# Decays computed sequence by sequence, B loaded in halves, fillers rearranged, and two gathers moved, in a fused scan and expert kernel

## The chip, the core and the metric

The kernel runs on one core of a Trainium2 chip. The metric is the device time of one execution in microseconds (us), median of several runs. The profiled execution comes with a span, from the first to the last instruction, which is a little shorter than the device time.

## What is computed

Two blocks stand one behind the other. The first is a selective state-space scan over 4 sequences, 8 heads, 768 positions, head size 32 and state size 16; the second sends each of the 3072 tokens to one of 8 experts by a hash of its id.

```python
# scan, per sequence b and head h, in chunks along the positions
cum   = cumsum(log(clip(a, 1e-6, 1)))            # inside a chunk
M     = (C @ B.T) * exp(cum_i - cum_j) * causal
y     = M @ x + (C @ state) * exp(cum_i)
state = exp(cum_last) * state + sum_j exp(cum_last - cum_j) * B_j x_j
# bridge: tokens are (b, position), features are (head, head_dim), so 3072 x 256
e     = token_id * 2654435761 % 8
out   = relu(y @ w1[e]) @ w2[e]                  # w1 256 x 1024, w2 1024 x 256
```

## The kernel before

All of the order is written by hand (`tc.manual_schedule`): each engine executes its instructions in the order in which the program names them, so a waiting instruction holds back everything behind it on that engine.

**Start.** The decays `a` of all four sequences come in one transfer (L90) into `a_t`, 96 partitions by 32 rows (sequence, head) by 8 positions. Behind it on the queue of SyncE come B and C of sequence 0 (`load_bc(0)`, L97, tile `bc`), x of sequence 0 (`load_x(0)`, L110, tile `xall`, two transfers) and B and C of sequence 1. While these land, GpSimd builds masks, VectorE and ScalarE put zeros in the unused halves of `xall` (`clear_x`, L150), and TensorE multiplies constants (`spin`, L193, tile `y_ps`), which keeps it active. Then the decay chain runs once for all four sequences: clamp (L386, VectorE), logarithm (L388, ScalarE), running sum (L392, VectorE), a small matmul (L397), an addition (L399), two exponentials (L401 and L402, giving `fac`), and an expansion for the steps (`totx`, L411, GpSimd). The factors `step` and `step2` come from `steps()` (L435): four small matmuls and three exponentials, called inside `turn_b(0)`.

**Scan.** For each sequence, `rows` multiplies B or C by its factors (on VectorE for sequence 0, L465, and on GpSimd for the others, L469); `turn_b` and `turn_c` transpose the result on TensorE (L499) and copy it out of PSUM on ScalarE (L505, L512, L515); `turn_c` also builds `cp` on GpSimd (L522). `turn_steps` transposes B back in blocks (L482; `bs`). `states` multiplies by x (L538) and carries the state forward on VectorE (L543, L547). `blocks` spreads the states over heads (L562). `grams` (L574, masked by `causal` into `m` on VectorE, L578) and `outputs` (L590, L597) give 128 tokens at a time, which ScalarE copies (L600) and SyncE writes to the tensor `y_tokens` (L601). The loop over `gc` (L638, 24 steps, 6 for each sequence) takes one output block per step and puts between them the preparation of the next sequence. `clear_x` for sequences 1 and 2 runs on ScalarE at steps 3, 5, 9 and 11 (L664). The routing (which expert, which place) is a generator `routing()` (L235); `next(todo)` puts one piece of it into the order of VectorE, a few per step (L665). It reads small tables that GpSimd fills (`tabs`, `keyc`, the `iota` tiles, L419 to L433).

**Experts.** The last steps of the scan gather the first two tiles of tokens (`gather_first`, L620, at step 17) and transpose them (`turn_x`, L616, at steps 22 and 23). Expert group 0 is then computed directly (`up` L854, `down` L865), while GpSimd gathers the tokens of the next groups (L605, tile `xg`) and forms sums of weights (`add_weights`, L736, tile `s`), `turn_next` transposes the gathered tokens (L884, copied by ScalarE into `xT`, L731), and `mix_x` (L761, tile `xmix`, VectorE) prepares group 1. Groups 1 to 7 use a scheme with seven products in place of eight (L795, L824). Results are transposed (L874) and scattered to the output (L713). The lines L900 to L920 order the passage into group 1.

Of the kernel before, what the change touches and what calls it, by code (L numbers as in the profile page):

```python
# [20 lines left out]
def kernel(  # L21
# [68 lines left out]
    nc.sync.dma_start(out=a_t, in_=a.rearrange("b h (p r) -> p (b h) r", r=RS))  # L90
# [3 lines left out]
    def load_bc(b):  # L94
        t = aload.tile([NR, 2, H, RS, NS], F32, name="bc")
        for i, src in ((0, B), (1, C)):
            nc.sync.dma_start(out=t[:, i].rearrange("p h r n -> p h (r n)"),  # L97
                              in_=src[b].rearrange("h (p r) n -> p h (r n)", r=RS))
        bcs[b] = t
# [16 lines left out]
    load_bc(0)  # L116
    load_x(0)
    load_bc(1)

# [24 lines left out]

    ident = const.tile([P, P], F32)
    make_identity(nc, ident)
    ones = const.tile([P, P], F32)
    nc.vector.memset(ones, 1.0)

    def clear_x(i, q, scalar):  # L150
        o = xall[q * HL:(q + 1) * HL, i, :, :, 1 - q].rearrange("j h k d -> j (h k) d")
        if scalar:
            nc.scalar.activation(o, ones[q * HL:(q + 1) * HL, 0:1].unsqueeze(2).to_broadcast([HL, G * NU, D]), AF.Copy, scale=0.0)  # L153
        else:
            nc.vector.memset(o, 0.0)

    clear_x(0, 0, False)
    scrap = const.tile([P, 1], F32)
    nc.scalar.activation(scrap, ones[:, 0:1], AF.Ln)
    clear_x(0, 1, True)  # L160
# [28 lines left out]
    turn0 = const.tile([NR, BH, RS], F32)  # L189
    nc.vector.memset(turn0, 1.0)  # L190
    nc.vector.memset(turn0[:, :, 0:1], 0.0)

    def spin(n, width=2):  # L193

        t = ps_y.tile([P, 512], F32, name="y_ps")
        for _ in range(n):
            nc.tensor.matmul(out=t[:, 0:width * P].rearrange("p (w i) -> p w i", w=width), lhsT=ident,
# [37 lines left out]
    def routing():  # L235
# [4 lines left out]
        nc.vector.tensor_scalar(out=eid_i, in0=tok[:, :, 0], scalar1=E - 1, scalar2=None, op0=OP.bitwise_and)  # L240
        eid_r = route.tile([NCH, P], F32)
        nc.vector.tensor_copy(out=eid_r, in_=eid_i)
        e_ps = ps_g.tile([P, 2, 512], F32, name="gram")[:, 0, 0:NCH]
# [119 lines left out]
        for c in range(NCH):  # L363
# [18 lines left out]
    next(todo)  # L382
    spin(2)


    nc.vector.scalar_tensor_tensor(out=a_t, in0=a_t, scalar=1e-6, in1=ones[0:NR, 0:1].unsqueeze(2).to_broadcast([NR, BH, RS]),  # L386
                                   op0=OP.max, op1=OP.min)
    nc.scalar.activation(a_t, a_t, AF.Ln)  # L388
    next(todo)
    cum = apre.tile([NR, BH, RS], F32)  # L390
    flat = lambda t: t.rearrange("p c r -> p (c r)")
    nc.vector.tensor_tensor_scan(out=flat(cum), data0=flat(turn0), data1=flat(a_t), initial=0.0,  # L392
                                 op0=OP.mult, op1=OP.add)
    next(todo)
    tot = cum[:, :, RS - 1]
    rel_ps = ps_t.tile([P, 512], F32, name="tp")
    nc.tensor.matmul(out=rel_ps[0:NR, 0:BH], lhsT=rel_w.rearrange("p k r -> p (k r)"), rhs=tot, start=True, stop=True)  # L397
    rel = apre.tile([NR, BH, RS], F32)
    nc.vector.tensor_tensor(out=rel, in0=cum, in1=rel_ps[0:NR, 0:BH].unsqueeze(2).to_broadcast([NR, BH, RS]), op=OP.add)  # L399
    fac = apre.tile([NR, 2, BH, RS], F32)  # L400
    nc.scalar.activation(fac[:, 0], rel, AF.Exp, scale=-1.0)  # L401
    nc.scalar.activation(fac[:, 1], rel, AF.Exp)  # L402
    next(todo)
    spin(2)

# [3 lines left out]
    nc.vector.memset(step2, 0.0)  # L409

    nc.gpsimd.tensor_copy(out=totx, in_=tot.unsqueeze(2).to_broadcast([NR, BH, NS]))  # L411
# [3 lines left out]
                            compare_op=OP.is_ge, fill=0.0, base=0, channel_multiplier=-1)  # L415
    nc.gpsimd.tensor_copy(out=causal[HL:P], in_=causal[0:HL])


    tabs = route.tile([P, 2, V], F32)  # L419
    for v in range(V):  # L420
        nc.gpsimd.memset(tabs[:, 0, v:v + 1], float(CAP - CAPS[v]))
        nc.gpsimd.memset(tabs[:, 1, v:v + 1], float(BEG[v] - 1 - (CAP - CAPS[v])))

# [683 lines left out]
```

## Time and profile before

Median of three runs: 255.59 us (253.53 to 255.78). The profiled run took 253.97 us, with a span of 252.2 us at a mean granted TensorE clock of 0.983.

| engine | busy us | share of the span |
|---|---|---|
| TensorE, matmul (PE) | 239.0 | 95% |
| TensorE, weight load (PEld) | 220.6 | 87% |
| VectorE (DVE) | 167.8 | 67% |
| GpSimd (POOL) | 135.7 | 54% |
| ScalarE (ACT) | 111.8 | 44% |

TensorE is the engine that sets the time. In a view of the profile by stages, it is busy for the whole of nearly every stage from 24 us on, until about 230 us. Where it is less busy, or runs at a lower clock, are the first 24 us: of 0 to 6 us it is busy 4.34, of 6 to 12 us 4.42, and of 18 to 24 us 4.58 us. (Some of that is the constant multiplication of `spin`.) A busy share says nothing on the clock: the profile gives the granted TensorE clock of each stage separately, 1.00 being the full one.

The transfers of the start, in order of their issue on SyncE, with the time from issue to landing that the profile gives for each:

| transfer | KB | issued at us | us to landing | landed at us |
|---|---|---|---|---|
| a, all sequences | 96 | 0.80 | 3.8 | 4.6 |
| B, sequence 0 | 384 | 1.25 | 5.7 | 7.0 |
| C, sequence 0 | 384 | 3.17 | 5.8 | 9.0 |
| x, sequence 0, first half | 384 | 3.75 | 7.0 | 10.8 |
| x, sequence 0, second half | 384 | 4.5 | 9.7 | 14.2 |
| B, sequence 1 | 384 | 8.71 | 7.7 | 16.4 |
| C, sequence 1 | 384 | 11.04 | 6.7 | 17.7 |

### The profile page before, as it was taken

The numbers are of one execution on the slowest core, as the hardware profiler recorded it, in microseconds if no ns is written. First come the engines' busy times: TensorE is split into PE (matmuls) and PEld (weight loads), VectorE is DVE, ScalarE is ACT, GpSimd is POOL, SyncE is SP. The second block draws the span as 40 slices with busy tenths as digits, with TensorE's granted clock in tenths as the row PEclk, the third lists the DMA queues.
The fourth block names the chain that finished last, engine by engine and source line by source line (L and its number), as shares of the span: only waits on it lengthen the run. The fifth ranks groups of instructions, "written<-read, shape, count | busy, mean of one in ns | idle before, by whom it ended". The sixth has DMA issues, their size and how long they took to land.

```text
span 252.2 us, 6781 instructions
## 1 busy us (share of the span) xinstructions
PE 239.0 (95%) x2615; PEld 220.6 (87%) x2615; DVE 167.8 (67%) x378; ACT 111.8 (44%) x256; POOL 135.7 (54%) x207
## 2 busy tenths in 40 slices
PE   6798999999999999999999999999999999999990
PEld 4676888888887788999999999999999999999970
DVE  6866488698652058676974994996787697784400
ACT  6643887965441325424334344343443453342120
POOL 6683290955303984279348629908937925504043
PEclk9987999999999999999999999999999999999998
DMA  6976899987872129242551642354164241001011
GB/s 115 160 122 116 131 201 189 248 196 233 249 256 67 60 92 312 71 168 62 171 209 42 208 166 83 119 173 147 47 209 184 62 169 39 21 4 40 21 44 60
DMA packets 50837, 33.21 MB, mean 132 GB/s; under 512 B 29753, under 2 KB 47186, under 8 KB 50804
## 3 DMA queue, kind: packets, MB, share of 16 engines
q1 hardware_dynamic: 47024, 24.22, 36.9%
q0 software_dynamic: 2400, 6.43, 8.1%
q10 hardware_dynamic: 1380, 2.12, 2.6%
q8 instruction: 21, 0.34, 0.6%
q14 instruction: 12, 0.10, 0.1%
HBM read 26.47 MB, written 6.42 MB: 130 GB/s over the span
## 4 chain that ended last, share of the span: by engine, by line
PE 73%; issue 11%; DVE 5%; ACT 4%; POOL 3%; DMA 1%; POOLq 1%; ACTq 0%
PE o_ps L824 20%; PE sum L795 12%; PE rest L795 6%; PE gram L574 5%; PE y_ps L590 5%; PE y_ps L597 4%; PE more L795 3%; PE tp L482 3%; PE o_ps L865 3%; POOL out_dram L713 2%; PE tp L499 2%; PE tp L538 2%; PE turns L884 2%; PE turns L874 2%; DMA a_t<-in_a_dram 1%
## 5 line engine op out<-in xcount | busy, mean ns | idle before, releaser
L713 POOL DMA_INDIRECT out_dram<-o_sb,idx_out x25 | 25.9, 1038 | 64.2 <-ACT o_sb L731 59.0
L824 PE MATMUL o_ps<-mixed,s 128*128 128x210 f32 (+6 forms) x168 | 37.0, 331 | 0.0
L605 POOL DMA_INDIRECT xg<-y_tokens,idx_in x25 | 26.4, 1058 | 18.5 <-ACT hd L725 12.0
L824 PEld LDWEIGHTS o_ps<-mixed,s 128*128 128x128 f32 x168 | 27.9, 190 | 0.0
L522 POOL TENSOR_TENSOR cp<-ct,step 128x256 f32<-128x256 f32 x24 | 13.9, 613 | 22.4 <-ACT ct L512 22.4
L731 ACT ACTIVATE u<-sum 128x420 f32<-128x420 f32 (+6 forms) x28 | 14.0, 501 | 23.6 <-PE sum L795 22.9
L795 PE MATMUL sum<-xmix,s 128*128 128x210 f32 (+6 forms) x112 | 23.5, 332 | 0.0
L736 DVE TENSOR_TENSOR mixed<-hT,mixed 128x420 f32<-128x420 f32 (+6 forms) x28 | 21.1, 754 | 0.5
L736 DVE TENSOR_TENSOR hT<-u,rest 128x420 f32<-128x420 f32 (+6 forms) x28 | 15.8, 564 | 7.7 <-PE rest L795 7.4
L578 DVE TENSOR_TENSOR m<-gram,causal 128x512 f32<-128x512 f32 x24 | 16.4, 685 | 5.9 <-PE gram L574 5.9
L808 DVE SCALAR_TENSOR_TENSOR mixed<-hT 128x420 f32<-128x420 f32 (+6 forms) x28 | 18.2, 691 | 1.0
L795 PEld LDWEIGHTS sum<-xmix,s 128*128 128x128 f32 x112 | 18.3, 189 | 0.6 <-issue 0.5
L731 ACT ACTIVATE o_sb<-turns 128x256 f32<-128x256 f32 x23 | 8.8, 384 | 20.5 <-PE turns L874 20.5
L600 ACT ACTIVATE y_sb<-y_ps 128x256 f32<-128x256 f32 x24 | 9.3, 388 | 17.9 <-PE y_ps L597 14.4
L597 PE MATMUL y_ps<-xall,m 128*64 128x64 f32 x384 | 16.8, 227 | 0.1
L574 PE MATMUL gram<-ce,bt 32*64 32x128 f32 x384 | 16.8, 288 | 0.0
L736 DVE TENSOR_TENSOR hT<-p,more 128x420 f32<-128x420 f32 (+6 forms) x14 | 7.9, 564 | 13.2 <-PE more L795 13.2
L731 ACT ACTIVATE xT<-turns 128x256 f32<-128x256 f32 x23 | 8.8, 384 | 17.2 <-PE turns L884 17.2
L590 PE MATMUL y_ps<-up,cp 128*64 128x128 f32 x176 | 16.2, 292 | 0.0
L731 ACT ACTIVATE p<-sum 128x420 f32<-128x420 f32 (+6 forms) x14 | 7.0, 501 | 20.3 <-PE sum L795 20.3
L597 PEld LDWEIGHTS y_ps<-xall,m 128*64 128x64 f32 x384 | 15.5, 141 | 0.6 <-ACT xall L153 0.6
L469 POOL TENSOR_TENSOR rows<-bc,fac 96x256 f32<-96x256 f32 x24 | 15.5, 675 | 0.8 <-DMA bc<-in_B_dram 0.7
(218 smaller groups left out, 581.5 us busy)
## 6 DMA issues: line engine op xcount, KB each, us to landing
w1odd<-in_moe_w_dram SPq DMA_DIRECT2D x8, 512.0 KB, 4.3
w2odd<-in_moe_w_dram SPq DMA_DIRECT2D x8, 512.0 KB, 4.4
y_tokens<-y_sb SPq DMA_DIRECT2D x24, 128.0 KB, 4.1
w1even<-in_moe_w_dram SPq DMA_DIRECT2D x6, 512.0 KB, 5.0
w2even<-in_moe_w_dram SPq DMA_DIRECT2D x6, 512.0 KB, 4.6
xall<-in_x_dram SPq DMA_DIRECT2D x12, 192.0 KB, 4.4
bc<-in_B_dram SPq DMA_DIRECT2D x4, 384.0 KB, 5.6
bc<-in_C_dram SPq DMA_DIRECT2D x4, 384.0 KB, 6.7
```

The costliest lines, as they stand in the source:

```text
L469: eng.tensor_tensor(out=t.rearrange("p r (h n) -> p h r n", h=H)[:, h:h + 2], in0=bcs[b][:, i, h:h + 2], in1=fac[:, i, hs].unsqueeze(3).to ...
L574: nc.tensor.matmul(out=gram[q * HL:(q + 1) * HL, g, u * P:(u + 1) * P], lhsT=bts[b][rr, 2 * c + u], rhs=ces[b][rr, :, 2 * c + u], start=Tr ...
L578: nc.vector.tensor_tensor(out=m.rearrange("p g u e i -> p g (u e i)"), in0=gram[:, :, 0:2 * P], in1=causal.rearrange("p (g x) i -> p g (x ...
L590: nc.tensor.matmul(out=y_ps[u * HL:(u + 1) * HL, :, q], lhsT=cps[b][:, q, k], rhs=ups[b][:, k].rearrange("p g (e d) -> p (g e) d", e=2), s ...
L597: nc.tensor.matmul(out=y_ps[u * HL:(u + 1) * HL, h], lhsT=m[:, g, u, e], rhs=xs[b][:, h, k], start=(k == 0 and h == 0), stop=(h == G - 1), ...
L605: nc.gpsimd.indirect_dma_start(out=dst, out_offset=None, in_=y_dram[0:n, :], in_offset=bass.IndirectOffsetOnAxis(ap=idx, axis=0), bounds_c ...
L713: st = nc.gpsimd.indirect_dma_start(out=out[:], out_offset=bass.IndirectOffsetOnAxis(ap=idx, axis=0), in_=src, in_offset=None, bounds_chec ...
L731: nc.scalar.activation(o, i, AF.Copy)
L736: eng.tensor_tensor(out=o, in0=i, in1=j, op=op)
L795: nc.tensor.matmul(out=self.banks[name][:, e * n:(e + 1) * n], lhsT=wt, rhs=mv, start=start and e == 0, stop=True, skip_group_check=True)
L808: nc.vector.scalar_tensor_tensor(out=t[:, o], in0=h[:, i], scalar=0.0, in1=h[:, k], op0=OP.max, op1=OP.subtract)
L824: nc.tensor.matmul(out=oP[v][o][:, e * n:(e + 1) * n], lhsT=wt, rhs=mv[:, c * n:(c + 1) * n], start=(j == 0 and c == 0 and i in (1, 3, 6, ...
```

## The change

The change has five parts. (1) `a` is loaded and turned into factors in three pieces: sequence 0, sequence 1, and sequences 2 and 3. The first piece goes ahead of everything, the others behind B and C of sequence 0 and behind B and C of sequence 1. The decay chain becomes a generator, `decays`, run for each piece; the clamps of the later pieces are on GpSimd. `steps` is called for each piece too. (2) B of sequence 0 is loaded in two halves by position, so that `rows` can begin on the first. (3) One activation table with logarithm and exponential is loaded at the start. (4) TensorE's fillers use a tile that is ready earlier, come as two groups of three, and two short ones are put between the first transposes; one `clear_x` goes from ScalarE to GpSimd, half of `cp` of sequence 0, the tables of the routing, and the second half of the states of sequence 0 go later in the order (the tables are filled behind the clamp of sequences 2 and 3, where the diff has `next(dec[2])` ahead of the loop). (5) At the passage to the experts, the first two token tiles are transposed one step earlier, the fourth tile of group 1 is transposed after the last `up`, and two gathers for group 2 are issued between the two halves of GpSimd's sums.

```diff
+    def load_a(b0, b1, eng):
+        eng.dma_start(out=a_t[:, b0 * H:b1 * H], in_=a[b0:b1].rearrange("b h (p r) -> p (b h) r", r=RS))
-    nc.sync.dma_start(out=a_t, in_=a.rearrange("b h (p r) -> p (b h) r", r=RS))
+    load_a(0, 1, nc.sync)
...
-            nc.sync.dma_start(out=t[:, i].rearrange("p h r n -> p h (r n)"),
-                              in_=src[b].rearrange("h (p r) n -> p h (r n)", r=RS))
+            n = RS // 2 if (b, i) == (0, 0) else RS
+            for r in range(0, RS, n):
+                nc.sync.dma_start(out=t[:, i, :, r:r + n].rearrange("p h r n -> p h (r n)"),
...
     load_bc(0)
+    load_a(1, 2, nc.sync)
     load_x(0)
     load_bc(1)
+    load_a(2, NB, nc.sync)
...
     clear_x(0, 0, False)
-    scrap = const.tile([P, 1], F32)
-    nc.scalar.activation(scrap, ones[:, 0:1], AF.Ln)
-    clear_x(0, 1, True)
+    nc.scalar.preload_act_table_set("natural_log_exp_and_others")
...
-            nc.tensor.matmul(out=t[:, 0:width * P].rearrange("p (w i) -> p w i", w=width), lhsT=ident,
+            nc.tensor.matmul(out=t[:, 0:width * P].rearrange("p (w i) -> p w i", w=width), lhsT=ones,
...
+    def decays(b0, b1):
...
+        eng = nc.gpsimd if b0 else nc.vector
+        eng.tensor_scalar(out=a_t[:, bh], in0=a_t[:, bh], scalar1=1e-6, scalar2=1.0, op0=OP.max, op1=OP.min)
+        yield
+        nc.scalar.activation(a_t[:, bh], a_t[:, bh], AF.Ln)
+        yield
+        nc.vector.tensor_tensor_scan(out=flat(cum[:, bh]), data0=flat(turn0[:, 0:n]), data1=flat(a_t[:, bh]), initial=0.0,
+                                     op0=OP.mult, op1=OP.add)
+        yield
+        tot = cum[:, bh, RS - 1]
+        rel_ps = ps_y.tile([P, 512], F32, name="y_ps")
+        nc.tensor.matmul(out=rel_ps[0:NR, 0:n], lhsT=rel_w.rearrange("p k r -> p (k r)"), rhs=tot, start=True, stop=True)
+        nc.gpsimd.tensor_copy(out=totx[:, bh], in_=tot.unsqueeze(2).to_broadcast([NR, n, NS]))
+        yield
+        nc.vector.tensor_tensor(out=rel[:, bh], in0=cum[:, bh], in1=rel_ps[0:NR, 0:n].unsqueeze(2).to_broadcast(sh), op=OP.add)
+        nc.scalar.activation(fac[:, 0, bh], rel[:, bh], AF.Exp, scale=-1.0)
+        nc.scalar.activation(fac[:, 1, bh], rel[:, bh], AF.Exp)
...
+    dec = {b: decays(b, min(2 * b, NB) if b else 1) for b in (0, 1, 2)}
+    next(dec[0])
+    next(dec[0])
+    next(todo)
+    next(dec[0])
+    next(dec[0])
+    next(todo)
+    next(dec[0], None)
+    spin(3)
...
+    next(dec[1])
     nc.gpsimd.tensor_copy(out=causal[HL:P], in_=causal[0:HL])
+    clear_x(0, 1, False, nc.gpsimd)
...
             if (b, i, r0) == (0, 0, RS // 2):
-                steps()
+                spin(1, 1)
+            elif (b, i, r0) == (0, 1, 0):
+                steps(0, 1)
+                next(todo)
+            elif (b, i) == (0, 1):
+                spin(1, 1)
...
+    next(dec[1])
     turn_c(0, True)
     next(todo)
     turn_steps(0, 0)
+    next(dec[1])
+    next(todo)
     grams(0)
-    states(0, 0)
+    next(todo)
+    states(0, 0, lambda: [next(dec[1], None) for _ in range(2)])
     blocks(0, 2, UH + 1)
     turn_steps(0, 1)
+    next(todo)
     rows(1, 0, nc.gpsimd)
+    put_steps(0, 8)
     rows(1, 1, nc.gpsimd)
+    next(dec[2])
...
-        if gc == 0:
-            states(0, 1)
+        if gc == 1:
+            steps(1, 2)
+        elif gc == 7:
+            steps(2, NB)
...
-                turn_b(nb)
+                turn_b(nb, (lambda: states(0, 1)) if b == 0 else None)
...
-        for _ in range((1, 2, 1, 0, 1, 0, 2, 2, 2, 0, 1, 0, 2, 2, 2, 1, 1, 0, 0, 1)[gc] if gc < 20 else 0):
+        for _ in range((1, 0, 0, 2, 1, 1, 2, 2, 2, 0, 1, 0, 2, 2, 2, 1, 1, 0, 0, 1)[gc] if gc < 20 else 0):
             next(todo, None)
+        if 0 < gc < 5:
+            next(dec[2], None)
...
-        elif gc > 21:
-            turn_x(gc - 22, (ps_t, "tp", 512), nc.vector.tensor_copy)
+        elif 20 < gc < 23:
+            turn_x(gc - 21, (ps_t, "tp", 512), nc.vector.tensor_copy)
...
-    for j in range(2):
-        take(add_weights(1, j, 0), 4)
+    take(add_weights(1, 0, 0), 4)
+    for k in new_tiles(2)[:2]:
+        gather(k)
+    take(add_weights(1, 1, 0), 4)
...
     for i in range(FP):
         up(0, i)
+        if i == 7:
+            turn_next(next(xs1))
+            mix_x(1)
         if i > 2:
             down(0, i - 3)
-        for _ in range((0, 0, 0, 0, 1, 1, 2, 0)[i]):
+        if 3 < i < 7:
             turn_next(next(xs1))
         if i == 5:
-            for k in new_tiles(2):
+            for k in new_tiles(2)[2:]:
                 gather(k)
-        if i == 6:
-            mix_x(1)
```

## The prediction, made before the change was run

> **What bounds the kernel now.** I read the stages first, then the chain that ended last, then the waits of the engine that sets the time. From 24 to 230 us TensorE is busy nearly throughout; time can only be won in front of that stretch, in its few gaps, or in its clock. The view by stages (us, then busy time and instruction count of PE, PEld, DVE, ACT and POOL, granted clock, DMA share, GB/s) shows two stretches at half clock:
>
> ```profile
> 10.00:11.00 1.00, 0.77 (x9) 0.59 (x8) 0.96 (x4) 0.85 (x4) 0.72 (x7) 1.00 1.27 178
> ...
> 13.00:14.00 1.00, 1.00 (x23) 0.88 (x20) 0.56 (x1) 1.00 (x3) 1.00 (x2) 0.50 1.15 187
> ...
> 19.00:20.00 1.00, 0.52 (x14) 0.42 (x14) 0.07 (x1) 0.36 (x2) 1.00 (x2) 1.00 0.00 0
> ...
> 23.00:24.00 1.00, 1.00 (x20) 0.94 (x16) 0.93 (x6) 0.00 (x0) 0.00 (x0) 0.50 0.78 127
> ```
>
> The chain of waits of the start (start us, length us, what) says what TensorE was late for:
>
> ```profile
> 0.80 3.76 DMA a_t<-in_a_dram
> 4.59 0.42 DVE a_t L386
> ...
> 7.14 0.43 ACT fac L401
> 7.60 1.06 DVE rows L465
> ...
> 13.36 1.06 PE gram L574 x16
> 14.42 1.15 PE tp L538 x48
> ...
> 17.61 0.48 DVE bs L485
> ...
> 19.90 0.49 PE tp L499 x4
> ```
>
> Decays until 7.57, transposes and copies until 13.36, states at 14.42, and a gap before the transposes of sequence 1 at 19.90. The chain does not name the transfers that arrived just in time: the second half of x landed at 14.2 us, and the first use of it (L538) is at 14.35; B of sequence 1 landed at 16.4 and its `rows` began at 16.56. ScalarE's timeline in the loop is nearly closed:
>
> ```profile
> 27.20 0.38 ACT L600 ACTIVATE y_sb<-y_ps 128x256 f32<-128x256 f32 x1 [1.00 <-PE y_ps L597]
> ...
> 34.60 0.39 ACT L600 ACTIVATE y_sb<-y_ps 128x256 f32<-128x256 f32 x1 [0.34 <-PE y_ps L597]
> 35.01 1.48 ACT L153 ACTIVATE xall<-ones 64x1536 f32<-64x1536 f32 x1
> ```
>
> Its clearing ends at 36.49 and the outputs of step 6 begin at 36.54: here ScalarE, not TensorE, ends the chain. Last, TensorE's waits from 60 to 110 us are three in all (engine, line, waited for: us, times, longest):
>
> ```profile
> PE turns L884 <- ACT xT L731: 0.9, 2, 0.5
> PE sum L854 <- DVE xT L618: 0.5, 1, 0.5
> ```
>
> **What the Trainium skill says.** "TensorE: Matmul & The Clock Gate", section on the HAM clock gate: the array's clock is halved unless recent activity was high, judged in free-running windows of about 3.4 us. The trace agrees on the halving and the length (11.81 to 15.02, 21.93 to 25.14), not on a simple busy share: PE was busy 2.82 us in the 3.4 us before the first, 2.17 between 5.0 and 8.4, and only the former was followed by half clock. "ScalarE: Activation LUTs", section on table sets: one set holds both exponential and logarithm. The trace shows two loads of 1.28 us each, of which the second (5.47 to 6.75) ended before `rel` was ready at 7.12. "DMA: Bandwidth & Descriptors", section on small descriptors: a fixed 3 cycles per packet, 11 cycles for 256 B. That makes 22 against 19 for two halves of 512 B, 16% (an estimate; no row here has 256 B pieces). "SBUF — State Buffer", section on who interferes with whom: an instruction of VectorE with two inputs contends with a GpSimd instruction that reads, not with one that only writes. So a clearing moved to GpSimd should leave VectorE's multiplications alone; no run so far shows it.
>
> **The change part by part.**
>
> *The first factors.* The pieces of `a` are 32 B long and took about 1.8 us of transfer (some 65 GB/s from 2.0 to 3.8 us, where B begins). A quarter takes 0.45, so it lands 1.35 earlier, at 3.2 in place of 4.56. The chain then has four times less per instruction. From the rows (0.42, 0.42, 0.69, 0.35, 0.42, 0.43 at 256 elements) and small ones of the same kind (0.17 to 0.21), I estimate clamp 0.2, logarithm 0.24, sum 0.29, matmul 0.3, addition 0.2, exponential 0.24, with gaps 0.2: 1.7, so factors at 4.9 in place of 7.57. The single table hides nothing new now, but keeps the shorter chain from meeting the second load. So the decay chain alone gains 2.7.
>
> *Does that reach TensorE?* B of sequence 0 comes 1.35 earlier for the missing `a`, less 16% of its 1.7 us of transfer, 0.3: 5.9 in place of 6.95, and its first half 1 us before that. C also comes about 1.0 earlier, at 8.0. `rows` of C then run 8.0 to 9.6, the transposes end near 10.2, and `ct`, which ended at 12.28, near 10.7. So the two grams and the first half of `bs` are ready by 12. But L538 needs x. On the queue in front of x stands half of `a` less than before (-0.9), and the halves of B (+0.3): x lands at 13.6 in place of 14.2 (bounds: 13.3 with no cost of the halves, 14.2 if they cost 0.9). **So only 0.6 of the 2.7 pass**, and B of sequence 1 likewise comes at 15.8 in place of 16.4. The clear (1.4 on GpSimd by its 64x512 memset of 0.52), behind the masks and the clamp of sequence 1 (0.2 to 0.35, which waits until about 8 for its piece), ends near 10.5, before any output.
>
> *Sequence 1.* GpSimd needs 2.75 from the start of `rows` to the fourth instruction (1.33 and three of 0.48 in the trace), so from 15.9 to 18.6, and TensorE's transposes follow at 18.7. Putting the second states behind the first batch of them lets TensorE use the rows at once; before, the copy of `bs` at 17.61 and a gap of 0.71 put them to 19.90. The group is L499 0.5, L538 0.7, L499 0.4: the gram of step 2 comes at 20.3 at full clock, at 21.0 to 21.6 if half clock falls on it, in place of 21.51. The outputs of step 0 are done near 17, so TensorE waits some 1.7 us ahead of 18.7, and so I count on half clock until about 21.9, as long as before but 3.3 earlier. Then the outputs of step 1 end at 22.9 in place of 24.13: 1.2 gained.
>
> *ScalarE in the loop.* It gets three exponentials for `step` (0.5 by L441 and L444: 0.21, 0.41), the logarithm for sequences 2 and 3 (0.29), and their two exponentials (0.56): 1.35. Half of it goes before step 2, where it waited 1.00 for TensorE; so `y_sb` of step 2 begins at 22.9 + 2.5 = 25.4, 1.8 earlier than 27.20. The exponentials of step 4 replace the wait of 0.34. **At the outputs of step 6 the start has gained 1.8**; at full clock throughout it would be 2.2, as ScalarE then has no gap left.
>
> *A new wait.* `keyc` is filled only behind `rows` of sequence 1 (8 times 0.48, plus 0.85), two pieces of `cp` (1.2), a clamp (0.3) and 18 memsets (0.6): near 22.8. VectorE's `key` waits for it, and `m` of step 2 is queued behind, done near 24.4. The outputs that need it come at 25 if step 1 ends at 22.9: nothing; at full clock it costs the rest above 2.2.
>
> *The passage.* The early `turn_x` lets VectorE's copy go beside the outputs of step 23: 0.5 (0.52 in the trace). The fourth `turn_next` behind the last `up` takes away one of the two waits on ScalarE's copy: 0.5 (0.47). `xmix` then is ready at 90.9 less 0.5, ahead of L795 at 92.18 less 1.0. The gathers of group 1 land 2.7 to 3.5 us from issue, the first at 82.4, and its transpose would stand at 82.78 less 0.5: no wait, or 0.1. The two early gathers hold the second sums by 2.6 us, to 92.6, while these are used at about 104: nothing. **Sum here 1.0.** The seven groups and the end stay as they are, bound by TensorE.
>
> Forecast: 255.6 - 1.8 - 1.0 = **252.8 us**.
>
> **Rivals.** (B) The fillers hold the clock, and the landings move by more than 0.6, since the queue is relieved also of the waiting behind it: B of sequence 1 a further 1.2 earlier, half clock 0.6 less: 252.8 - 1.8 = 251.0. For it: 4.5 us of one queue's issue time go into x alone; against: x is bound by its 128 B pieces (786 KB from 7.4 to 12.7 us), which stay. (C) A transfer that is hidden anyway: halves of B cost 0.9, x lands at 14.2 as before, B of sequence 1 too, and only the order (0.2) and the passage (1.0) gain: 254.4. For it: x at 14.2 against its use at 14.35; against: 48 KB less of the smallest pieces ahead of it. (D) Slower: the additions to ScalarE lie in full on the closed stretch (+1.35), and VectorE's wait for `keyc` delays `m` (+0.9, if GpSimd's contention stretches its rows), with nothing from the start and the passage's 1.0: 256.8. For it: the closed timeline above; against: the 1.00 gap in it.
>
> **How the numbers follow.** Forecast 0.5, B 0.25, C 0.17, D 0.08. The likeliest is 252.8. The range goes from B, with 0.2 for a full clock, to C, with 0.5 for a first gather that TensorE waits for: 250.8 to 254.9. Faster by over 1% means under 253.03: all of B and six tenths of the forecast, 0.55. Slower by over 1% would need D twice over: 0.06. The rest, 0.39, is within 1%.
>
> **What would show it.** The first exponential done near 4.9; L538 starting when x lands, near 13.6; `rows` of sequence 1 at 15.9; half clock in one stretch around 18.7 to 21.9; the outputs of step 6 at 34.7; no wait of L854 on `xT`, and one in place of two of L884. It is wrong if x lands no earlier, if VectorE's `key` holds up `m`, or if TensorE waits at a place that the trace before does not show.

## The result, and the profile after

The changed kernel takes **257.44 us** (median of 6 runs, 256.43 to 258.29), the kernel before in the same comparison 254.95 us (6 runs, 253.53 to 255.78). The ratio is **1.0104**, 95% interval 1.0064 to 1.0144: slower by some 2.5 us, where 252.8 us and a gain were forecast. The profiled execution has a span of 255.8 us, against 252.2. In some executions every one of these kernels runs slower as a whole; the ratios leave these out, the medians do not, and each group of experiments has its own timing of the kernel before (medians from 253.19 to 253.90 us).

The view by stages of the changed kernel (us, then busy time and instruction count of PE, PEld, DVE, ACT and POOL, granted clock, DMA share, GB/s), in the stretches that were shown of before:

```profile
10.00:11.00 1.00, 0.76 (x28) 0.62 (x25) 0.94 (x3) 0.97 (x4) 0.92 (x2) 1.00 1.63 141
...
13.00:14.00 1.00, 0.91 (x22) 0.57 (x25) 0.64 (x2) 0.00 (x0) 0.74 (x2) 0.50 1.17 224
...
18.00:19.00 1.00, 1.00 (x12) 1.00 (x13) 0.97 (x4) 1.00 (x4) 1.00 (x3) 0.50 0.03 8
19.00:20.00 1.00, 1.00 (x16) 0.93 (x15) 1.00 (x2) 0.22 (x2) 1.00 (x2) 0.72 0.00 0
...
23.00:24.00 1.00, 1.00 (x28) 0.96 (x26) 0.03 (x1) 0.84 (x5) 0.94 (x23) 1.00 0.43 70
```

Half clock now comes in one stretch from 12.73 to 19.56, as long as the two of before together (11.62 to 15.03 and 21.86 to 25.27 by the granted clock; the prediction has their ends up to 0.2 us off). The gap of TensorE between 19 and 20 is gone. The chain of waits (start us, length us, what) says where the start went, and, 15 us later, what took its place:

```profile
2.54 5.03 DMA bc<-in_C_dram
...
7.66 1.33 DVE rows L476 x2
...
9.51 1.35 DVE own L463
...
12.76 0.29 DVE mask L262
...
13.09 0.34 PE gram L267
...
13.61 1.43 PE tp L561 x48
...
32.27 0.28 DVE st L572
32.55 0.17 DVE at_g L292
32.74 0.41 DVE tabx L296 x2
...
34.18 0.59 DVE m L603
...
35.48 0.19 DVE rel L418
35.69 0.31 ACT fac L419
36.00 0.20 ACT fac L420
...
36.49 1.49 ACT xall L164
37.98 0.04 issue
38.03 0.69 PE y_ps L622 x16
```

The factors are early, and TensorE reaches the states (L561, L538 before) 0.8 us earlier. But the chain then runs through VectorE: pieces of the routing (`at_g`, `tabx` and what follows) stand behind the states of sequence 1 and ahead of the mask `m` of a step and of `rel` of sequences 2 and 3, for whose exponentials ScalarE waits, with the copy of step 5 and a clearing of 1.49 us behind them. The outputs of step 6, which began at 36.54, begin at 38.03. In ScalarE's timeline the wait for `rel` is this:

```profile
34.34 0.47 ACT L498 ACTIVATE bs<-tp 128x384 f32<-128x384 f32 x1
35.69 0.31 ACT L419 ACTIVATE fac<-rel 96x128 f32<-96x128 f32 x1 [0.89 <-DVE rel L418]
...
36.11 0.36 ACT L625 ACTIVATE y_sb<-y_ps 128x256 f32<-128x256 f32 x1
36.49 1.48 ACT L164 ACTIVATE xall<-ones 64x1536 f32<-64x1536 f32 x1
```

The starts of the copies `y_sb`, one for each step, serve as time marks for the whole scan (us). Three kernels of the experiments below are set beside them; c2 is the kernel before with part 5 and with the clearings of sequences 1 and 2 moved to GpSimd (up to step 2 its program is otherwise that of the kernel before):

| step | before | after | e8_counts | c3 | c2 |
|---|---|---|---|---|---|
| 0 | 19.00 | 19.83 | 18.83 | 18.56 | 19.03 |
| 1 | 24.17 | 23.14 | 22.14 | 22.07 | 22.56 |
| 2 | 27.20 | 26.08 | 25.56 | 25.77 | 25.05 |
| 3 | 30.36 | 29.21 | 28.70 | 28.90 | 28.21 |
| 4 | 32.11 | 32.68 | 30.74 | 30.95 | 31.16 |
| 5 | 34.60 | 36.11 | 33.23 | 33.44 | 33.65 |
| 6 | 37.27 | 38.76 | 36.70 | 36.62 | 36.38 |
| 8 | 42.27 | 44.30 | 42.26 | 42.17 | 41.39 |
| 12 | 52.39 | 54.63 | 52.73 | 52.64 | 51.93 |
| 23 | 76.06 | 80.00 | 76.71 | 76.62 | 76.26 |

The changed kernel is 1.03 us ahead at step 1 and 1.15 at step 3; **between steps 3 and 6 it loses 2.64 us**. Later, 1.66 us more go between steps 16 and 17 (65.35 to 69.55, 4.20 us in place of 2.54), where TensorE stands for 0.77 us and ScalarE for 2.06 with nothing shown that they wait for; e2_scan, e8_counts and c3 pass these steps in 2.54.

Part of the lead at step 1 belongs to the clock: the profile before had half clock from 21.86 to 25.27, while c2 and c3 had full clock through the whole scan. e2_scan (below) has the scan of the changed kernel, also at full clock. It is 0.15 us ahead of c2 at step 1 (22.41), but 1.32 behind at step 2 (26.37) and 1.96 behind at step 6 (38.34), where c2 is also spared ScalarE's clearings. c3, too, is 0.49 ahead of c2 at step 1 and 0.72 behind at step 2. At like clock, then, these single profiles show 0.15 to 0.49 us of the start's gain at step 1 and none at step 2. There `m` stands on VectorE behind the routing's `key`, which waits for `keyc`, and TensorE waits for `m`, for 0.93 us in e2_scan and 0.66 in c3:

```profile
25.64 0.69 PE L622 MATMUL y_ps<-xall,m 128*64 128x64 f32 x16 [0.93 <-DVE m L603]
...
25.04 0.69 PE L621 MATMUL y_ps<-xall,m 128*64 128x64 f32 x16 [0.66 <-DVE m L602]
```

The passage shows the third piece: TensorE's waits from 60 to 110 us (engine, line, waited for: us, times, longest) are

```profile
PE tp L561 <- issue: 0.8, 2, 0.4
PE turns L933 <- DMA xg<-y_tokens,idx_in: 0.7, 1, 0.7
PE turns L933 <- ACT xT L780: 0.5, 1, 0.5
PE sum L903 <- ACT hd L774: 0.5, 1, 0.5
```

The wait for `xT` ahead of the first sums is gone, and one of two ahead of the turns, as planned. A wait for `hd` (the hidden values of group 0, written by ScalarE) and one for a gather of group 2 have come: 0.99 us saved (0.52 and 0.47), 1.19 added (0.45 and 0.74). From the copy of step 20, behind which part 5 begins to move things, to the first transposes of group 0's results it is 35.76 us before (71.33 to 107.09) and 36.11 after (74.92 to 111.03): in this profile the passage gains nothing.

### The profile page after: what moved, and what is told of

Read it like the earlier page. It is cut to its first block, busy times and chain, and to the rows that moved or that the text cites. A ratio compares the mean times of both kernels' runs of the same rounds, so it can differ in the third digit from the quotient of the medians.

```text
span 255.8 us, 6810 instructions
## 1 busy us (share of the span) xinstructions
PE 240.7 (94%) x2621; PEld 222.1 (87%) x2621; DVE 169.0 (66%) x381; ACT 110.3 (43%) x265; POOL 139.9 (55%) x213
## 3 DMA queue, kind: packets, MB, share of 16 engines
q10 hardware_dynamic: 1380, 2.12, 2.7%
## 4 chain that ended last, share of the span: by engine, by line
PE 62%; DMA 15%; issue 8%; POOL 5%; DVE 4%; ACT 2%; SPq 2%; POOLq 0%; DVEq 0%; ACTq 0%
PE o_ps L873 21%; PE sum L844 12%; DMA out_dram<-o_sb,idx_out 7%; PE rest L844 6%; PE gram L599 4%; PE y_ps L615 4%; PE y_ps L622 4%; PE more L844 3%; DMA xg<-y_tokens,idx_in 3%; POOL s L785 2%; DMA xall<-in_x_dram 2%; POOL xg L630 2%; PE tp L561 2%; DMA bc<-in_C_dram 2%; PE tp L493 2%
## 5 line engine op out<-in xcount | busy, mean ns | idle before, releaser
L546 POOL TENSOR_TENSOR cp<-ct,step 128x256 f32<-128x256 f32 x24 | 14.5, 638 | 15.8 <-ACT ct L531 15.7
L603 DVE TENSOR_TENSOR m<-gram,causal 128x512 f32<-128x512 f32 x24 | 16.3, 682 | 2.9 <-PE gram L599 2.8
L780 ACT ACTIVATE xT<-turns 128x256 f32<-128x256 f32 x23 | 8.8, 383 | 18.4 <-PE turns L933 18.4
L785 DVE TENSOR_TENSOR oT<-us,o_ps 128x210 f32<-128x210 f32 (+13 forms) x21 | 8.3, 425 | 11.0 <-ACT us L780 11.0
```

Source lines behind the costliest of these rows:

```text
L603: nc.vector.tensor_tensor(out=m.rearrange("p g u e i -> p g (u e i)"), in0=gram[:, :, 0:2 * P], in1=causal.rearrange("p (g x) i -> p g (x ...
L780: nc.scalar.activation(o, i, AF.Copy)
L785: eng.tensor_tensor(out=o, in0=i, in1=j, op=op)
```

## The experiments

My first theory was that the scan's part loses and the passage's part gains, and that inside the scan the loss is VectorE's order of work in steps 3 to 6. The letter V in the expectations stands for it. Rivals: the late x of sequence 1 (X), the GpSimd clearing beside VectorE at 9.4 us, ScalarE's load at step 6, the splitting of the chain as such, and, formed later, the small matmuls that now lie in the loop (M). Ratios are to the kernel before, timed on the same chip; 0.001 is 0.25 us.

**The two halves of the change.** e1_passage is the kernel before with part 5 alone:

```diff
-        elif gc > 21:
-            turn_x(gc - 22, ...)
+        elif 20 < gc < 23:
+            turn_x(gc - 21, ...)
...
+        if i == 7:
+            turn_next(next(xs1))
+            mix_x(1)
...
-    for j in range(2):
-        take(add_weights(1, j, 0), 4)
+    take(add_weights(1, 0, 0), 4)
+    for k in new_tiles(2)[:2]:
+        gather(k)
+    take(add_weights(1, 1, 0), 4)
```

> The kernel before with part 5 alone (earlier transposes of the first two tiles, fourth transpose behind the last product, two gathers amid the sums). Theory S (the loss is made in the scan: x of sequence 1 late, ScalarE's stretch): the passage is worth nothing or a little, 254.3 to 255.3 us against 254.95. Theory P (the passage makes the loss: in the changed kernel's trace a gather of group 2 landed 7.0 us after issue and TensorE waited 0.74 us for it): 255.7 to 256.5. The prediction's own step: 254.0.

e2_scan is the changed kernel with these lines undone, parts 1 to 4 alone.

> The changed kernel with part 5 undone, so the scan's parts alone. Theory S: still slower than before by 2 to 3 us, 257 to 258. Theory P: 255.5 to 256.5, since about one us of the loss goes away.

Measured: e1_passage 253.85 us, 0.9979 (0.9947 to 1.0012); e2_scan 256.15 us, 1.0103 (1.0068 to 1.0138). The scan's parts carry the loss. By the ratio the passage gains 0.5 us, half of the 1.0 forecast, and its interval includes zero. Its waits in e1_passage show why it isn't the whole:

```profile
PE turns L884 <- ACT xT L731: 0.5, 1, 0.5
PE turns L884 <- DMA xg<-y_tokens,idx_in: 0.5, 1, 0.5
```

The second line is the first gather of group 1, issued at 79.98 and needed at 83.48: TensorE now comes before it. The profile of e2_scan also settles a question on the clock: TensorE was granted full clock throughout its first 28 us, and its `y_sb` of step 1 began at 22.41 (after: 23.14), of step 6 at 38.34 (38.76). The half clock moves with the run and is worth 0.42 us at step 6 between these two profiles; it does not make the loss.

**The early clearing.** e3_clear_act puts the clearing of half of `xall` back on ScalarE:

```diff
-    clear_x(0, 1, False, nc.gpsimd)
...
     next(dec[0], None)
+    clear_x(0, 1, True)
     spin(3)
```

> The changed kernel with the clearing of the second unused half of x (sequence 0) back on ScalarE, behind the two exponentials, where ScalarE is idle from 5.1 to 6.9 us. If GpSimd's clearing is what stretched VectorE's copy of own from 0.23 to 1.35 us and the small routing copies beside it, and so kept TensorE waiting 1.46 us for mask ahead of the states: own at 0.2 to 0.4 us, mask before 11.5, states of sequence 0 begin when x lands (13.0 to 13.5), and the time falls by 0.3 to 1.0. If x is the only bound there: states begin at the same 13.5 and the time stays within 0.3.

Measured: 255.29 us, 1.0070 (1.0039 to 1.0102), which overlaps the changed kernel's interval. What the clearing does is plain from the rows. VectorE's timeline of the changed kernel, beside its GpSimd clearing from 9.40 to 10.77:

```profile
9.10 0.38 DVE L462 TENSOR_TENSOR hm<-hm 128x4 f32<-128x4 f32 x1
9.51 1.35 DVE L463 COPY own<-hm 128x128 f32<-128x128 f32 x1
9.65 1.21 DVE L255 COPY eid<-gram 128x24 f32<-128x24 f32 x1
10.92 0.58 DVE L257 TENSOR_SCALAR late<-eid 128x9 f32<-128x9 f32 x1
```

and of c3 (below), in which the clearing is on ScalarE as in e3_clear_act:

```profile
9.49 0.38 DVE L461 TENSOR_TENSOR hm<-hm 128x4 f32<-128x4 f32 x1
9.91 0.23 DVE L462 COPY own<-hm 128x128 f32<-128x128 f32 x1
10.05 0.18 DVE L255 COPY eid<-gram 128x24 f32<-128x24 f32 x1
10.26 0.17 DVE L257 TENSOR_SCALAR late<-eid 128x9 f32<-128x9 f32 x1
```

The copy was blocked until the clearing was done. That held `mask`, for which TensorE (L267) waited 1.46 us in the changed kernel; most of that wait, though, stood where x would have been waited for: in c3, where `mask` came earlier, TensorE waited 0.96 us for x instead and went on with the states at 13.94, and in the changed kernel L561 began at 13.54. So the blocking is shown, its price in device time (0.0034 by the two medians) is not.

**The late x of sequence 1.** TensorE waited 1.13 us for it at 28.7. e4_x1_early issues it before the loop:

```diff
     load_a(2, NB, nc.sync)
+    for i in range(4):
+        load_x(1, i)
...
-        for i in range(4) if gc == 0 else ():
-            load_x(1, i)
```

> The changed kernel with the four loads of x of sequence 1 issued behind the last piece of a, ahead of the loop, so that no write of y stands in front of them. Theory S: TensorE's wait for x of sequence 1 (1.1 us at 28.7) goes, and 1.0 to 1.7 us with it: 255.7 to 256.5. If ScalarE's stretch has no gap behind it and takes up the slack: less than 0.5 gained, 257 and more.

Measured: 256.71 us, 1.0110 (1.0068 to 1.0152): no gain is measured, though the two intervals leave room for about 1.3 us. The wait was gone, and another stood in its place (TensorE's waits from 20 to 45 us, e4_x1_early):

```profile
PE y_ps L624 <- DVE m L605: 1.1, 2, 0.9
PE y_ps L624 <- ACT xall L166: 0.6, 1, 0.6
```

The transfer had been late beside a VectorE that was later. That rival finds no support, and the row points at `m`, queued behind the routing on VectorE.

**VectorE's order.** e8_counts gives the changed kernel the old distribution of the routing pieces over the steps:

```diff
-        for _ in range((1, 0, 0, 2, 1, 1, 2, 2, 2, 0, ...
+        for _ in range((1, 2, 1, 0, 1, 0, 2, 2, 2, 0, ...
```

> The changed kernel with one tuple put back: the pieces of the routing are taken at the steps of the kernel before (1, 2, 1, 0, 1, 0 for the steps 0 to 5 in place of 1, 0, 0, 2, 1, 1). Theory V (VectorE's order makes the loss: in steps 3 and 4 the moved pieces and the late addition for sequences 2 and 3 stand ahead of m, hold ScalarE's exponentials by 1.6 us and then the clearing that the outputs of step 6 wait for): from the outputs of step 4 to those of step 5 in 2.5 to 3.0 us, not 3.4 to 4.1, and 1.0 to 1.6 us less than the changed kernel (about 1.005 of before). Theory X (x of sequence 1, late, is what costs): the time does not fall by more than 0.4, as that wait stays.

Measured: 254.26 us, **1.0047** (1.0022 to 1.0072). By the ratios this one tuple is worth 0.0057, more than half of the loss; from the two intervals I estimate 0.001 to 0.010. VectorE's timeline of e8_counts:

```profile
23.45 0.17 DVE L283 SCALAR_TENSOR_TENSOR key<-key,keyc 128x9 f32<-128x9 f32 x1 [1.75 <-POOL keyc L677]
...
24.69 0.23 DVE L292 TENSOR_TENSOR at_g<-place,iota_v 128x81 f32<-128x81 f32 x1
...
32.07 0.27 DVE L418 TENSOR_TENSOR rel<-cum,y_ps 96x128 f32<-96x128 f32 x1
```

`at_g` runs at 24.69 where the changed kernel has it at 32.47; VectorE has room there (in the kernel before it waited 1.53 and 1.06 us for grams between 24 and 29). `rel` comes at 32.07 in place of 35.39, and the copy of step 5 at 33.23 in place of 36.11. The wait for `keyc` is longer than in the changed kernel (1.75 against 1.30), and the kernel is faster: what sets the two apart is the move of the pieces, not the wait for the tables. The wait still costs something: TensorE waits 0.38 us for `m` at step 2 of e8_counts. No run puts the tables back where they were, so their price in device time stays open.

**ScalarE's load.** e6_clear1_pool takes the two 1.5 us clearings of steps 3 and 5 from ScalarE and puts them on GpSimd behind the tables:

```diff
-        if gc in (3, 5, 9, 11):
+        if gc in (9, 11):
...
     one_up = count("one_up", [P, 1], [[0, 1]], 1, 1)
+    clear_x(1, 0, False, nc.gpsimd)
+    clear_x(1, 1, False, nc.gpsimd)
```

> The changed kernel with the two clearings for sequence 1 moved from ScalarE (steps 3 and 5) to GpSimd behind its tables, where it is idle from 24.5 to 28.5 us. If ScalarE's stretch is the bound of steps 3 to 6: the wait of the outputs of step 6 for the clearing (0.6 us) goes and the time falls by 0.6 to 1.2 (about 1.006 of before). If VectorE's order is: the wait moves to m or to the copy of y, and less than 0.5 is gained.

Measured: 255.01 us, 1.0081 (1.0050 to 1.0112). A quarter of the loss by the medians, with overlapping intervals. The copy of step 6 begins at 37.70 in place of 38.76; TensorE's wait is now 0.9 us for `m` (L603) instead of 0.64 for `xall`.

**The splitting.** e5_one_chain loads and computes all decays at once, and leaves the other parts:

```diff
-    load_a(0, 1, nc.sync)
+    load_a(0, NB, nc.sync)
...
-    dec = {b: decays(b, min(2 * b, NB) if b else 1) for b in (0, 1, 2)}
+    dec = {0: decays(0, NB)}
```

> The changed kernel with the decays of all four sequences in one chain at the start, as before: one load of a ahead of all, one clamp on VectorE, no piece of decays in the loop, one call of steps. All else as changed. If the late pieces of decays cost more in the loop than the early factors bring at the start (theory V, and the 0.54 us of matmuls of steps 2 and 3 at step 7): 0.5 to 1.5 us faster than the changed kernel, with the outputs of step 1 later by 0.5 to 1.5. If the pieces by sequence are what is good in the change: slower than the changed kernel, 1.013 and more of before.

Measured: 257.26 us, 1.0154 (1.0105 to 1.0203), the slowest of all: it waited 2.0 us for `eid_r` (the routing's first piece, now behind the longer chain), 1.9 for x of sequence 1 and 2.4 for `m`. So no loss by the splitting as such is shown in this order; without the splitting the ratio is even higher, but the intervals overlap. The run doesn't restore the order of before, so it says nothing on that.

**Four edits together.** c1 has e3_clear_act, e4_x1_early, e6_clear1_pool and e8_counts at once.

> The changed kernel with four edits together: the clearing of sequence 0 on ScalarE, x of sequence 1 loaded ahead of the loop, the routing's pieces at their old steps, the clearings of sequence 1 on GpSimd. If these four places are the loss and the start's gain (1 to 1.5 us at the outputs of step 1) is real, it is kept to the end: 252.0 to 253.0, 0.993 to 0.997 of before. If a further cost hides behind them (the half clock, the matmuls of step 7): 0.997 to 1.003.

Measured: 254.09 us, 1.0039 (1.0015 to 1.0064). Its copy of step 6 begins at 35.62, 1.65 us before that of the kernel before and 0.76 before that of c2, which also had full clock and also clears on GpSimd: a lead is there, but beside c2 it is less than half as large. It is also 1.08 us ahead of e8_counts, whose ScalarE still does the clearing of step 5. At step 23 it is at 76.64 against 76.06: the lead has been given back between steps 7 and 23, with 0.95 us in one stop of TensorE at step 12 that no run explains. Between steps 7 and 8 alone 0.55 us go, and there the step matmuls of sequences 2 and 3 stand in the loop.

**The small matmuls.** e10_more_pe is the kernel before with the same four small matmuls that the change has in steps 1, 3 and 7, as extra work that nothing uses:

```diff
         outputs(gc)
+        if gc in (1, 7):
+            more_ps = ps_y.tile([P, 512], F32, name="y_ps")
+            for j in range(1 + gc // 7):
+                nc.tensor.matmul(out=more_ps[:, j * NU:(j + 1) * NU], lhsT=totx[...], rhs=step_w, ...)
...
+        if gc == 3:
+            nc.tensor.matmul(out=more_ps[0:NR, 0:2 * H], lhsT=rel_w[...], rhs=cum[:, 0:2 * H, RS - 1], ...)
```

> The kernel before with four small matmuls of the decays and steps repeated inside the loop, where the changed kernel has them (one with 128x12-class output in step 1, one of the running totals in step 3, two in step 7); their results are used by nothing. Theory M (the change moved TensorE work out of the idle start into a loop that TensorE paces, and my sum priced it at nothing): the changed kernel's records give these groups 0.39, 0.34 and 0.61 us, so 1.0 to 1.3 us longer than before, ratio 1.004 to 1.005. Rival (the loop has gaps in which they fit, the rest of the loss is elsewhere): under 0.4 us, ratio at most 1.0015.

Measured: 255.09 us, **1.0069** (1.0048 to 1.0090), 1.2 to 2.3 us longer. The rows of the added work in e10_more_pe (out<-in, shapes, count | busy us, mean ns | idle before):

```profile
L647 PE MATMUL y_ps<-step_w,totx 96*128 96x12 f32 x6 | 1.0, 266 | 0.0
L672 PE MATMUL y_ps<-cum,rel_w 96*96 96x16 f32 x2 | 0.3, 246 | 0.0
```

1.3 us of matmuls, each recorded twice. Where the profile isolates them, at step 7, they are not hidden: from the copy of step 7 to that of step 8 it is 3.08 us in place of 2.54, for two matmuls recorded with 0.61. Not all of the longer time is theirs, though: from step 20 to the first transposes of group 0's results this profile takes 36.66 us in place of 35.76, with a wait of 0.65 for `hd` that the kernel before has not, and nothing was added there. In the changed kernel the same groups stand at L425 and L415; the kernel before did all of this work (L438, L397) ahead of the loop. The expectation's upper end is passed, the rival's 1.0015 excluded.

e11_no_steps23 tries the reverse: e8_counts without the step matmuls and exponentials of sequences 2 and 3, whose steps are preset to a constant, so that their outputs are left uncomputed.

```diff
-        elif gc == 7:
-            steps(2, NB)
...
     nc.gpsimd.memset(step2, 0.0)
+    nc.gpsimd.memset(step[:, 2:NB], 0.5)
```

> The changed kernel with the old order of the routing pieces (as e8_counts, 254.3 us, ratio 1.0047) and without the two step matmuls and three exponentials of sequences 2 and 3 in step 7; their steps are preset by one GpSimd memset, so the outputs of sequences 2 and 3 are left uncomputed in that respect. Theory M: 0.6 us less than e8_counts, ratio 1.0020 to 1.0028. Rival: within 0.2 us of e8_counts, ratio 1.004 to 1.005.

Measured: 254.07 us, 1.0035 (1.0010 to 1.0060), against 1.0047 (1.0022 to 1.0072): half of the expected difference, and not to be told from none. In the profiles, though, the place is clear: from the copy of step 7 to that of step 8 it is 2.55 us as in the kernel before, and 3.09 in e8_counts. Step 23 came at 75.80 against 76.71; 0.55 us of that lead is lost again in the passage (35.97 us from step 20 to the first transposes, 35.42 in e8_counts).

**The gathers.** e7_gathers_back is the changed kernel with the gathers of group 2 where they were:

```diff
-    for k in new_tiles(2)[:2]:
-        gather(k)
...
-            for k in new_tiles(2)[2:]:
+            for k in new_tiles(2):
```

> The changed kernel with the gathers of the second group back behind all of the weight sums, as before; everything else changed. If the wait of 0.74 us at the first turn of the second group in the changed kernel's trace is a loss that the earlier issue brings, 0.3 to 0.7 us less, ratio 1.007 to 1.009. If it is only the gap that the sums leave anyway, no difference: ratio 1.009 to 1.012, and if the earlier issue does help, 1.012 or more.

e12_turns_only is the kernel before with part 5 but without the early gathers.

> The kernel before with the passage to the experts of the changed one, but the gathers of the second group left where they were, behind the weight sums. If the earlier gathers are a loss (the changed kernel ran 0.0025 shorter without them) and the earlier turns a gain of about 1.0 us (the two waits of 0.5 us gone): 0.994 to 0.997, below the 0.9979 of e1_passage. If the gathers cost nothing: 0.997 to 0.999.

Measured: e7_gathers_back 255.65 us, 1.0079 (1.0052 to 1.0106), 0.0025 below the changed kernel; e12_turns_only 253.20 us, 0.9992 (0.9972 to 1.0012), not below the 0.9979 of e1_passage but above it. The two point opposite ways, and both are within the intervals: **no effect of the gathers' place is shown**. In e7_gathers_back TensorE waited for the gather 1.0 us, in the changed kernel 0.7. The wait is there in either order, as soon as TensorE arrives earlier.

**Versions meant to beat both.** c2 is e1_passage with the clearings of sequences 1 and 2 on GpSimd:

```diff
     rows(1, 1, nc.gpsimd)
+    clear_x(1, 0, False, nc.gpsimd)
+    clear_x(1, 1, False, nc.gpsimd)
...
-        if gc in (3, 5, 9, 11):
-            clear_x(1 + gc // 9, gc % 6 // 5, True)
+        if gc in (6, 7):
+            clear_x(2, gc - 6, False, nc.gpsimd)
```

> A version meant to beat both: the kernel before with the passage to the experts of the changed one (e1_passage, ratio 0.9979) and the clears of the x buffers of sequences 1 and 2 on GpSimd, idle there, in place of four 1.5 us ScalarE instructions in steps 3, 5, 9 and 11. In the changed kernel the clears of sequence 1 alone gave 0.0023. Theory (ScalarE is late at step 6 and is asked less): ratio 0.994 to 0.997. Rival (a GpSimd memset holds VectorE up as the one at 9.4 us in the changed kernel did): 0.998 or more.

Measured: 253.78 us, 1.0015 (0.9993 to 1.0037). It doesn't win; 6 us of ScalarE's instructions taken away bring nothing that can be measured. In the kernel before, ScalarE's clearing ahead of the outputs of step 6 ends the chain of waits there, and yet its removal is worth nothing that these runs show.

c3 undoes three suspected losses of the changed kernel together: e8_counts, e3_clear_act and e7_gathers_back.

> The changed kernel with three losses undone together: the old order of the routing pieces (0.0057 alone), the early clear of the x buffer on ScalarE instead of GpSimd (0.0034 alone), the second group's gathers in the old place (0.0025 alone). If the losses are independent they add: 1.0104 - 0.0116, ratio 0.998 to 1.000, and the change then has the gain that was forecast less its matmuls in the loop. If they are the same slack counted thrice (each moves the loop's pace, which then finds its next limit): 1.002 to 1.005.

Measured: 254.26 us, **1.0014** (0.9995 to 1.0033), between the two answers. Of the changed kernel's 0.0104, 0.0090 is gone, where the single differences add up to 0.0116: they mostly add. What remains of the scan's gain shows in the table: 2.10 us ahead of before at step 1, 1.16 at step 5, 0.65 at step 6, 0.10 at step 8, and 0.56 behind at step 23. Most of the 2.10 goes with the clock: beside c2, at full clock like c3, it is 0.49 at step 1, and 0.72 behind at step 2. In the passage c3 then stands 1.66 us for the first gather of group 2, the longest wait of its loop and passage:

```profile
99.15 0.41 PE L932 MATMUL turns<-ident,xg 128*128 128x128 f32 x2 [1.66 <-DMA xg<-y_tokens,idx_in]
```

From step 20 to the first transposes it takes 36.25 us, against 35.42 in e8_counts, which keeps the early gathers. A version with the other two losses undone and the early gathers kept was not run. None of the versions is faster than the kernel before by more than its interval.

## Why the prediction was wrong, step by step

*The first factors and the landings: right.* The first exponential, forecast at 4.9, ended at 4.91 (the second at 5.06); C forecast at 8.0, landed 7.57; x at 13.6, landed by 13.5; L561 at 13.6, began 13.54; `rows` of sequence 1 at 15.9, began 16.08. "Only 0.6 of the 2.7 pass" was right (0.8): in c3 and c1 TensorE waits for x there, 0.96 and 0.78 us. Two of the times came by other causes than forecast: in the changed kernel itself TensorE waited for `mask`, and `rows` of sequence 1 for its late factors (L419), not for B.

*The half clock: wrong in place, small in effect.* Forecast 18.7 to 21.9, came 12.73 to 19.56, twice as long. "TensorE: Matmul & The Clock Gate", section on the HAM clock gate, says that the window is free-running and that the same kernel varies from run to run. The runs agree: e2_scan, whose start is that of the changed kernel, had full clock in its first 28 us. How little a head start by the clock is worth shows in the profile of e10_more_pe, which had full clock from 21.86 to 25.27 where the kernel before had not: 1.61 us ahead of it at step 2 (25.59), 0.27 at step 4 (31.84), after TensorE had waited 0.8 us for an x transfer. The prediction's reading of the windows before stands with the true ends: TensorE was busy 2.69 us in the 3.4 us before the first half clock and 2.12 before the second, but also 2.38 in a stretch (4.79 to 8.20) that full clock followed.

*Sequence 1 and step 1: the number nearly right, by luck of the clock.* The transposes came at 19.72, not 18.7, since TensorE did its work before them at half clock; in c3, at full clock, they came at 18.20. The outputs of step 1 gained 1.03 (forecast 1.2), against a profile that had half clock just there. Against c2 the same scan at full clock gains 0.15 (e2_scan).

*"`y_sb` of step 2 at 25.4" and "keyc held to cost nothing".* 26.08 was measured. The tables came at 23.84 (forecast 22.8), VectorE waited 1.30 and `m` stood behind, without holding TensorE in this profile. At full clock it does hold TensorE, as the prediction said ("at full clock it costs the rest above 2.2"): 0.66 us in c3, 0.93 in e2_scan. The sum left that out because it counted on half clock there. It isn't what e8_counts undoes, which waits 1.75 and is 1.4 us shorter.

*The step that failed first: the moved routing pieces, which my sum did not price.* I costed the additions of ScalarE in the loop (1.35) and did not lay VectorE's order out step by step. In the changed kernel seven instructions of the routing (32.5 to 34.2) stand between the states of sequence 1 and the `m` of step 5, for which TensorE waits, and four more ahead of the `rel` for which ScalarE waits. The loss from step 3 to step 6 is 2.64 us in the profile, where the forecast kept its gain of 1.8; undoing the order alone gives 0.0057, 1.4 us. Beside c2, e2_scan is 1.96 us behind at step 6 at like clock, and e8_counts, with half clock from 15.0 to 18.4, only 0.32. The outputs of step 6 came at 38.03, not 34.7.

*The second: the small matmuls, priced at nothing.* I counted ScalarE's exponentials of the later pieces, and left out the matmuls ahead of them. They moved from a start in which TensorE waited for other things into a loop that TensorE paces. e10_more_pe measures 1.2 to 2.3 us for 1.3 us of matmuls, part of it in the passage. For the two of step 7 the cost is shown from both sides: 0.54 us come with them (e10_more_pe) and 0.54 go without them (e11_no_steps23), between steps 7 and 8. The time of e11_no_steps23 as a whole does not show it beyond the intervals.

*The third: "a clearing moved to GpSimd should leave VectorE's multiplications alone".* "SBUF — State Buffer", section on who interferes with whom, which I cited for instructions with two inputs, says a few lines on that a VectorE copy in its two-port mode and GpSimd exclude each other for the whole instruction, whoever comes first. I took the one rule and not the other. Of VectorE's two-input instructions only `hm` ran into the clearing, for 0.08 us, and took the 0.38 us that it takes in c3, so the sentence itself was hardly tried; what it left out are the copies. The trace agrees with the other rule: `own`, a copy, 1.35 us beside the clearing and 0.23 without it. The price in device time is 0.0034 by medians, not shown beyond the intervals.

*The passage: right in mechanism, too large in size.* The two waits went as forecast. "The gather wait: no wait or 0.1" was 0.45 in e1_passage and 0.74 in the changed kernel (there a gather of group 2). Of 1.0 us, 0.5 was measured alone (interval -0.3 to 1.3), 0.2 without the gathers, and nothing inside the changed kernel: without the passage's part its ratio is 1.0103 (e2_scan), with it 1.0104.

*The rivals.* D (256.8, slower) came nearest to 257.44, by a cause of its own: not the additions of ScalarE (c2 and e6_clear1_pool take more away and bring little), but VectorE's order, and TensorE's additions. Its wait for `keyc`, priced at 0.9, is there at full clock (0.66 and 0.93). I gave D 0.08, and slower by over 1% 0.06; the chances leaned on a list of gains worked out in detail and on losses that were worked out only where I had looked.

*What stays open.* c3 is 0.4 us behind before, where the forecast was 2.8 ahead. The matmuls are up to 1.2 to 2.3 of that gap and the passage's shortfall 0.5 to 0.8 (estimates from e10_more_pe, e1_passage and e12_turns_only); the rest, from nothing to 1.5 us, is not settled. Its profile names candidates, none of them priced by a run of its own: 0.66 us for `m` at step 2, behind the tables; 0.70 and 0.43 us in which TensorE stands with no wait shown; 1.66 us for a gather.

## What to carry to other kernels

Work moved out of an idle start into a loop that one engine paces is not free because it is small: here 0.61 us of recorded matmuls took 0.54 at their step. Price each instruction of the pacing engine at its row's duration, and take from it only gaps that the trace shows. When a change reorders one engine's queue, write out for each step what stands ahead of the instruction that others wait for; a wait that is shorter can belong to a slower order, as `keyc` shows. A gain at the start must be followed to the end, and compared at like clock: here 2.1 us at step 1 were 0.6 us behind at step 23, and beside a profile with full clock they were 0.5 to begin with.

## What the runs showed of the hardware that I had not expected

- TensorE stood still with no wait shown, at the same instruction in many kernels: within the grams of step 12, behind the same few matmuls, for 0.29 us in the changed kernel, 0.51 in e2_scan, 0.43 in e8_counts and in c3, 0.95 in c1, and not at all in the kernel before. It doesn't take the changed scan: e1_passage, whose program up to step 20 is that of the kernel before, stands there 0.58 us. Nothing that I changed explains it. A second such place, in c3 and e8_counts alike, lies in step 6:

```profile
35.63 0.38 PE L614 MATMUL y_ps<-up,cp 128*64 128x128 f32 x2 [0.70 <-issue]
...
50.97 0.54 PE L598 MATMUL gram<-ce,bt 32*64 32x128 f32 x9 [0.43 <-issue]
```

  This one may well be the wait for ScalarE's clearing of step 5, which the changed kernel shows by name (0.64): in c3 the clearing ended at 35.33 and TensorE went on at 35.63, and in c1, where GpSimd clears, the stop is gone. The profile names no wait, so it isn't shown.
- A clamp of 96x64 elements took GpSimd 0.77 us, and one of 96x128 took 0.63: I had estimated 0.2 to 0.35, and size didn't set the time.
